# A fused attention and gated-MLP layer: the V weights on a second load queue, and the order of TensorE's first twelve microseconds

## Chip, cores and metric

The kernel runs on one core of one Trainium2 chip. The metric is the device time of one execution in microseconds (us), taken as the median of several runs. A profiled execution adds a trace, in which times are counted from the start of the span.

The engines are named as in the profile: PE is TensorE (matrix multiply; PEld is its weight load), DVE is VectorE, ACT is ScalarE, POOL is GpSimd, SP is SyncE. SPq and ACTq are the DMA issues made by SP and by ACT.

## What is computed

One input block `x` of 2048 rows by 512 columns (bf16) is layer-normalized. Two branches start from the normalized rows `xn`, and their results are added to `x`:

```python
def _A_ref(x, wqkv, wo):
    B, S, D = x.shape
    H = 32; Dh = D // H; W = 256
    qkv = (x @ wqkv).reshape(B, S, 3, H, Dh).transpose(2, 0, 3, 1, 4)
    q, k, v = qkv[0], qkv[1], qkv[2]
    scores = einsum("bhqd,bhkd->bhqk", q, k) * (Dh ** -0.5)
    idx = jnp.arange(S)
    mask = (idx[:, None] - idx[None, :] >= 0) & (idx[:, None] - idx[None, :] < W)
    p = softmax(where(mask, scores, -1e9))
    o = einsum("bhqk,bhkd->bhqd", p, v)
    return o.transpose(0, 2, 1, 3).reshape(B, S, D) @ wo

def _B_ref(x, w_gate, w_up, w_down):
    return ((x @ w_gate) * (x @ w_up)) @ w_down      # 1792 hidden columns

xn = layernorm(x)
out = x + _A_ref(xn, A_wqkv, A_wo) + _B_ref(xn, B_w_gate, B_w_up, B_w_down)
```

(The einsum and transpose wrappers of the reference are written out here.) The attention has 32 heads of 16 columns and a sliding window of 256 rows.

## The kernel before

**Tiling.** The 2048 rows are 16 blocks of 128, grouped in four chunks `T` of 512. Every product over the 512 input columns is a sum of four matmuls over 128 columns each (`k` = 0 to 3). For that the normalized block must stand with its columns in the partitions: `xnT`. In chunk 0 the four blocks are transposed by PE (four transposes of 128 by 128 a block into a PSUM tile `xTp`, which ACT copies to `xnT`, `norm_transpose`, L219 to L234); later chunks use DMA transposes.

**Order.** The program is written out in a fixed order, and each engine executes its own instructions in that order. `setup` (L82) issues all loads on SP's queue, in this order: x block 0, x block 1, x blocks 2 and 3 in one DMA, then the V, K and Q thirds of `Wqkv` (512 KB each), then halves of the gate and up weights, and so on. PE runs 40 matmuls on a zeroed tile `idle` meanwhile (`keep_busy`, L147); nothing reads their result.

`first_chunk` (L292) is the head of the kernel. For each block DVE computes the mean and variance (`norm_stats`, L193 and L194), POOL the reciprocal root (`norm_scale`, L206; DVE adds the epsilon for block 0, POOL for the others), and DVE the normalized block `xn` (`norm_apply`, L214). DVE's order is: statistics of blocks 0 and 1, normalization of 0, statistics of 2, normalization of 1, statistics of 3, normalization of 2. Then PE transposes block 0 and runs eight idle matmuls, and a loop over `b` transposes block `b + 1` and computes the V product of block `b` (`proj_v`, L258: four matmuls into one PSUM tile `vp`, then a copy to `V` by DVE, or by ACT for block 2). The normalization of block 3 is written after the V product of block 0, so that on DVE it comes behind that block's copy. After the loop come the first K and Q products (`proj_qk`, L275).

**The rest.** A loop over 64-row score pieces follows: scores on PE (L350), exponentials on ACT (L353), masks on POOL and DVE, sums over the values on PE (L473). Between these, gate and up products (L502, L513) and the projections of the next chunk are put as filler (`fill`); `PADS` adds no-ops to PE's stream after two of the steps, at most three to a piece of filler. Chunks 1 to 3 each begin with three gate and up pairs, then `down_phase`, which computes the down and output products of the chunk before (`psd`, L535 and L541) between wide score pieces (`B`).

**PSUM banks.** Eight banks hold matmul results. Banks 4 to 7 hold a score tile. The first four are handed out in rotation by `m_tile` (L77): `at_bank` is the next one. `down_phase` closes all and opens one bank for `psd` and three for `B`: `psd` gets bank 0 for the first block if `at_bank` is 0, else bank 3, and changes sides with each block:

```python
        late, high = None, 0 if self.at_bank == 0 else 1
        self.close_banks(5)
        for b in range(4):
            for name in ("ps_b", "ps_d") if b % 2 != high else ("ps_d", "ps_b"):
```

Of the kernel before, what the change touches and what calls it, by code (L numbers as in the profile page):

```python
# [7 lines left out]
BF16 = mybir.dt.bfloat16  # L8
# [28 lines left out]
class Kernel:  # L37
# [44 lines left out]
    def setup(self):  # L82
        nc, const, NT, NF = self.nc, self.const, self.NT, self.NF
        self.x = const.tile([128, NT, 512], BF16, name="x")
        self.Wqkv = const.tile([128, 4, 1536], BF16, name="Wqkv")
        self.Wo = const.tile([128, 4, 512], BF16, name="Wo")
        self.Wg = const.tile([128, 4, self.F], BF16, name="Wg")
        self.Wu = const.tile([128, 4, self.F], BF16, name="Wu")
        self.Wd = const.tile([128, NF, 512], BF16, name="Wd")
        xv = self.x_d.rearrange("(t p) d -> p t d", p=128)  # L90
        wq = self.w_d["qkv"].rearrange("(k p) n -> p k n", p=128)
        wg = self.w_d["g"].rearrange("(k p) n -> p k n", p=128)
        wu = self.w_d["u"].rearrange("(k p) n -> p k n", p=128)
        for lo, hi in ((0, 1), (1, 2), (2, 4)):
            nc.sync.dma_start(out=self.x[:, lo:hi, :], in_=xv[:, lo:hi, :])
        for lo in (1024, 512, 0):
            nc.sync.dma_start(out=self.Wqkv[:, :, lo:lo + 512], in_=wq[:, :, lo:lo + 512])
        h = self.F // 2
        for lo in (0, h):
            nc.sync.dma_start(out=self.Wg[:, :, lo:lo + h], in_=wg[:, :, lo:lo + h])  # L100
            nc.sync.dma_start(out=self.Wu[:, :, lo:lo + h], in_=wu[:, :, lo:lo + h])
            if lo == 0:
                nc.sync.dma_start(out=self.x[:, 4:8, :], in_=xv[:, 4:8, :])
        nc.sync.dma_start(out=self.Wd[:], in_=self.w_d["d"].rearrange("(f p) n -> p f n", p=128))
        wo = self.w_d["o"].rearrange("(c p) n -> p c n", p=128)
        for c in range(4):
            nc.sync.dma_start(out=self.Wo[:, c, :], in_=wo[:, c, :])
        for lo, hi in ((8, 10), (10, 12), (12, NT)):
            nc.sync.dma_start(out=self.x[:, lo:hi, :], in_=xv[:, lo:hi, :])

        self.idle = const.tile([128, 128], BF16, name="idle")
        nc.vector.memset(self.idle[:], 0.0)
        self.keep_busy(40)
        warm = const.tile([128, 1], F32, name="warm")
        nc.vector.memset(warm[:], 0.0)
        nc.scalar.activation(out=warm[:], in_=warm[:], func=ACT.Exp)
        ident = const.tile([128, 128], BF16, name="ident")
        nc.gpsimd.memset(ident[:], 0.0)
        nc.gpsimd.affine_select(out=ident[:], in_=ident[:], compare_op=ALU.not_equal, fill=1.0,
                                base=0, pattern=[[-1, 128]], channel_multiplier=1)  # L120
        self.ident = ident
        pi = const.tile([128, 1], I32, name="pi")
        nc.gpsimd.iota(pi[:], pattern=[[0, 1]], base=0, channel_multiplier=1)
        podd = const.tile([128, 1], I32, name="podd")
        nc.vector.tensor_scalar(out=podd[:], in0=pi[:], scalar1=4, scalar2=1,
                                op0=ALU.arith_shift_right, op1=ALU.bitwise_and)
        self.odd = const.tile([128, 1], F32, name="odd")
        nc.vector.tensor_copy(out=self.odd[:], in_=podd[:])
        self.even = const.tile([128, 1], F32, name="even")
        nc.vector.tensor_scalar(out=self.even[:], in0=self.odd[:], scalar1=-1.0, scalar2=1.0,  # L130
                                op0=ALU.mult, op1=ALU.add)
        self.mhalf = const.tile([128, 4], F32, name="mhalf")
        nc.gpsimd.memset(self.mhalf[:], -0.5)
        self.diag = const.tile([128, 64], BF16, name="diag")
        self.far = const.tile([128, 64], BF16, name="far")
        nc.gpsimd.memset(self.diag[:], BIG)
        nc.gpsimd.memset(self.far[:], BIG)
        for half in (slice(0, 64), slice(64, 128)):
            self.triangle(self.diag[half], True)
            self.triangle(self.far[half], False)  # L140
        self.xnT, self.Q, self.hT, self.OT = {}, {}, {}, {}
        self.K, self.V, self.VS = {}, {}, {}
        self.strips, self.parts, self.at = {}, {}, {}
        self.stock = []
        self.new_values()
# [73 lines left out]
    def norm_transpose(self, t, by_dma):  # L219

        nc = self.nc
        xn = self.xns.pop(t)
        T, b = divmod(t, 4)
        if b == 0:
            self.xnT[T] = self.chunk2.tile([128, 4, 4, 128], BF16, tag="xnT", name=f"xnT{T}")
        if by_dma:
            nc.sync.dma_start_transpose(out=self.xnT[T][:, b, :, :], in_=xn[:])
            return
        n = 2 if b == 0 else 4
        for lo in range(0, 4, n):  # L230
            ps = self.m_tile([128, n, 128], BF16, "xTp")
            for k in range(n):
                nc.tensor.transpose(ps[:, k, :], xn[:, 128 * (lo + k):128 * (lo + k) + 128], self.ident[:])
            nc.scalar.activation(out=self.xnT[T][:, b, lo:lo + n, :], in_=ps[:], func=ACT.Copy)  # L234
# [57 lines left out]
    def first_chunk(self):  # L292

        self.new_chunk(0)
        for b in range(2):
            self.norm_stats(b, 1)
            self.norm_scale(b, 1)
        for b in (0, 1, 2):
            self.norm_apply(b)
            if b < 2:  # L300
                self.norm_stats(b + 2, 1)
                self.norm_scale(b + 2, 1)
        self.norm_transpose(0, False)
        self.keep_busy(8)
        for b in range(4):
            if b < 3:
                self.norm_transpose(b + 1, False)
            self.proj_v(b, engine="act" if b == 2 else "dve")
            if b == 0:
                self.norm_apply(3)  # L310
        self.proj_qk(0, 0, 1, engine="dve")
        self.proj_qk(0, 0, 0, engine="act")
        self.swap_halves(0, self.nc.scalar)
        self.proj_qk(0, 1, 1, engine="dve")
# [491 lines left out]
```

## Time and profile before

| | us |
|---|---|
| Median of 3 runs | 262.15 (262.0 to 262.67) |
| The profiled execution, its own time | 262.46 |
| Its span | 260.6 |
| First x block: issued / statistics start | 0.79 / 3.03 |
| First transposes on PE (block 0) | 5.30 |
| First K product on PE, recorded start | 11.08 |

The span is the time from the first to the last recorded instruction; the execution's own time is 1.86 us longer. A PE record starts before its turn in the array, because matmuls are pipelined; in the chain of waits each piece begins where the one before it ends, so the same work stands there some 0.15 us later (the first K product at 11.24). Busy shares are averages over the whole span. What the change touches lies in the first twelve microseconds, so the timeline and the chain of that stretch are the views to read, together with each load's time from issue to landing.

### The profile page before, as it was taken

What the parts mean: (1) busy time and instruction counts of PE and PEld (TensorE: products, weight loads), DVE (VectorE), ACT (ScalarE), POOL (GpSimd) and SP (SyncE); (2) the same over time, 40 slices, a digit from 0 to 9 for tenths busy, and PEclk for the clock granted to TensorE, in tenths of its full rate; (3) what the DMA queues carried; (4) which work ended last, traced back from release to release, by engine and by line L of the source; (5) the groups of instructions that cost most, each with busy time, mean ns of one, the idle gap of its engine ahead of it and who ended that gap; (6) DMA issues with size and microseconds to landing.
All of it is one profiled execution on the core that took longest, in us unless ns stands there. A gap on an engine that the chain in (4) does not pass through costs nothing.

```text
span 260.6 us, 7774 instructions
## 1 busy us (share of the span) xinstructions
PE 256.4 (98%) x3170; PEld 120.1 (46%) x3170; DVE 169.0 (65%) x342; ACT 183.4 (70%) x167; POOL 114.7 (44%) x278
## 2 busy tenths in 40 slices
PE   8999999999999999999999999999999999999995
PEld 8444444444444544444544454444544445444453
DVE  6687898888836487347976468642895235948144
ACT  3377788888586788787756768879874877877500
POOL 6216242425356745343445764334242565543500
DMA  6999910120013220002001301000200100000002
GB/s 207 377 353 336 283 27 20 24 48 1 3 40 43 60 25 1 3 0 48 3 3 41 82 24 23 0 4 1 48 5 4 36 23 24 3 0 3 3 0 83
DMA packets 19426, 15.04 MB, mean 58 GB/s; under 512 B 7360, under 2 KB 19392, under 8 KB 19392
## 3 DMA queue, kind: packets, MB, share of 16 engines
q1 hardware_dynamic: 18848, 14.26, 19.7%
q8 instruction: 26, 0.43, 0.7%
q10 hardware_dynamic: 544, 0.30, 0.4%
q14 instruction: 8, 0.07, 0.1%
HBM read 9.70 MB, written 2.10 MB: 45 GB/s over the span
## 4 chain that ended last, share of the span: by engine, by line
PE 91%; DVE 7%; issue 1%
PE up L513 17%; PE gp L502 17%; PE psd L535 16%; PE qkp L275 10%; PE S L350 8%; PE acc L473 6%; PE vp L263 6%; PE psd L541 5%; PE L L535 2%; PE wps L151 2%; DVE at L479 2%; DVE hT L518 1%; DVE on L492 1%; PE B L350 1%; PE L L541 1%
## 5 line engine op out<-in xcount | busy, mean ns | idle before, releaser
L182 POOL TENSOR_SCALAR_AFFINE_SELECT P<-P 64x256 bf16<-64x256 bf16 x224 | 98.7, 441 | 122.4 <-ACT P L353 110.7
L353 ACT ACTIVATE P<-S 128x2048 bf16<-128x2048 f32 x66 | 123.8, 1876 | 23.3 <-PE S L350 22.4
L502 PE MATMUL gp<-xnT,Wg 128*128 128x512 bf16 x224 | 59.1, 380 | 0.0
L513 PE MATMUL up<-xnT,Wu 128*128 128x512 bf16 x224 | 59.0, 380 | 0.0
L518 DVE TENSOR_TENSOR hT<-up,gsb 128x512 bf16<-128x512 f32 x56 | 38.0, 683 | 24.7 <-ACT gsb L254 12.7
L535 PE MATMUL psd<-Wd,hT 128*128 128x512 bf16 (+1 forms) x210 | 47.8, 369 | 0.0
L448 DVE TENSOR_TENSOR P<-P,diag 128x512 bf16<-128x512 bf16 (+1 forms) x75 | 30.1, 401 | 16.0 <-ACT P L353 15.9
L254 ACT ACTIVATE gsb<-gp 128x512 bf16<-128x512 f32 x49 | 28.5, 596 | 9.5 <-PE gp L502 9.4
L535 PEld LDWEIGHTS <-hT 128*128 128x128 bf16 x238 | 21.6, 98 | 25.5 <-issue 3.1
L513 PEld LDWEIGHTS <-Wu 128*128 128x128 bf16 x224 | 20.6, 98 | 25.6 <-issue 2.7
L502 PEld LDWEIGHTS <-Wg 128*128 128x128 bf16 x224 | 20.5, 98 | 25.5 <-issue 2.9
L353 ACT ACTIVATE P<-B 128x1536 bf16<-128x1536 f32 (+2 forms) x18 | 17.8, 1022 | 17.7 <-PE B L350 10.8
L275 PE MATMUL qkp<-xnT,Wqkv 128*128 128x512 bf16 x128 | 29.8, 380 | 0.0
L350 PE MATMUL S<-Q,K 32*128 32x320 bf16 (+4 forms) x624 | 28.7, 255 | 0.0
L350 PEld LDWEIGHTS <-K 32*128 32x128 bf16 x720 | 11.4, 92 | 27.4 <-issue 26.5
L551 DVE TENSOR_TENSOR x<-psd,x 128x512 bf16<-128x512 f32 (+1 forms) x15 | 9.9, 665 | 20.8 <-PE psd L541 20.8
L479 DVE STREAM_TRANSPOSE at<-acc 128x512 f32<-128x512 f32 x30 | 19.1, 688 | 4.6 <-PE acc L473 4.6
L275 PEld LDWEIGHTS <-Wqkv 128*128 128x128 bf16 x128 | 11.8, 98 | 14.7 <-issue 1.6
L473 PE MATMUL acc<-P,VS 64*32 64x320 bf16 (+4 forms) x672 | 17.6, 253 | 0.0
L473 PE MATMUL acc<-P,V 64*32 64x320 bf16 (+4 forms) x672 | 17.2, 253 | 0.0
L473 PEld LDWEIGHTS <-VS 64*32 64x32 bf16 x720 | 15.4, 91 | 2.2 <-issue 1.5
L263 PE MATMUL vp<-Wqkv,xnT 128*128 128x512 bf16 x64 | 15.3, 380 | 0.0
(56 smaller groups left out, 191.3 us busy)
## 6 DMA issues: line engine op xcount, KB each, us to landing
out_dram<-x SPq DMA_DIRECT2D x15, 128.0 KB, 1.7
Wg<-in_B_w_gate_dram SPq DMA_DIRECT2D x2, 896.0 KB, 11.3
Wu<-in_B_w_up_dram SPq DMA_DIRECT2D x2, 896.0 KB, 12.4
Wd<-in_B_w_down_dram SPq DMA_DIRECT2D x1, 1792.0 KB, 16.7
Wqkv<-in_A_wqkv_dram SPq DMA_DIRECT2D x3, 512.0 KB, 6.3
x<-in_A_x_dram SPq DMA_DIRECT2D x2, 512.0 KB, 8.8
VS<-V SPq DMA_DIRECT2D x6, 144.0 KB, 2.6
x<-in_A_x_dram SPq DMA_DIRECT2D x3, 256.0 KB, 6.7
```

The costliest lines, as they stand in the source:

```text
L182: nc.gpsimd.affine_select(out=v, in_=v, pattern=pattern + [[1 if diag else -1, 64]], compare_op=ALU.is_ge if diag else ALU.is_gt, fill=0.0 ...
L254: nc.scalar.activation(out=out, in_=in_, func=ACT.Copy)
L263: nc.tensor.matmul(ps[:], lhsT=self.xnT[T][:, b, k, :], rhs=self.Wqkv[:, k, 1024:1536], start=(k == 0), stop=(k == 3))
L275: nc.tensor.matmul(ps[:], lhsT=self.Wqkv[:, k, lo:lo + 128], rhs=self.xnT[T][:, :, k, :], start=(k == 0), stop=(k == 3))
L350: self.nc.tensor.matmul(kw.pop("out"), start=True, stop=True, skip_group_check=True, **kw)
L353: self.nc.scalar.activation(out=out, in_=in_, func=ACT.Exp, scale=0.25)
L448: self.nc.vector.tensor_tensor(out=v, in0=v, op=ALU.min, in1=self.diag.unsqueeze(1).unsqueeze(1).to_broadcast([128, 4, n, 64]))
L473: nc.tensor.matmul(accs[par][32 * e:32 * e + 32, q:q + n], lhsT=v, rhs=P[rows, e, col:col + n], start=(i == 0), stop=(i == len(todo) - 1), ...
L502: nc.tensor.matmul(ps[:], lhsT=self.Wg[:, k, 128 * f:128 * f + 128], rhs=self.xnT[T][:, :, k, :], start=(k == 0), stop=(k == 3))
L513: nc.tensor.matmul(ps[:], lhsT=self.Wu[:, k, 128 * f:128 * f + 128], rhs=self.xnT[T][:, :, k, :], start=(k == 0), stop=(k == 3))
L518: nc.vector.tensor_tensor(out=self.hT[T, f][:], in0=ps[:], in1=self.gsb[:], op=ALU.mult)
L535: nc.tensor.matmul(ps, lhsT=self.hT[T, f][:, 128 * b:128 * b + 128], rhs=self.Wd[:, f, c0:c1], start=(f == 0), stop=False)
```

## The change

The V third of `Wqkv` (512 KB, one DMA) is issued by ACT instead of SP. A one-column memset by DVE into that third stands ahead of it, which the DMA has to wait for. The tile `idle` and its memset move to the start of `setup`, so that the order of DVE's memsets is `idle`, then the column, then `warm`.

In the head, eight idle matmuls after block 0's transposes become four. The V product of block 0 is split: its matmuls for `k` = 0 and 1 come ahead of block 1's transposes, those for 2 and 3 behind. Of block 2's V product, the matmul for `k` = 0 comes ahead of block 3's transposes. Block 3's transposes go to two tiles of two instead of one of four, so that ACT copies them in two instructions. After the V products of blocks 1 and 2, four no-ops each are put into PE's stream.

```diff
@@ setup @@
+        self.idle = const.tile([128, 128], BF16, name="idle")
+        nc.vector.memset(self.idle[:], 0.0)
         xv = self.x_d.rearrange("(t p) d -> p t d", p=128)
...
         for lo, hi in ((0, 1), (1, 2), (2, 4)):
             nc.sync.dma_start(out=self.x[:, lo:hi, :], in_=xv[:, lo:hi, :])
-        for lo in (1024, 512, 0):
+        nc.vector.memset(self.Wqkv[:, 0, 1024:1025], 0.0)
+        nc.scalar.dma_start(out=self.Wqkv[:, :, 1024:1536], in_=wq[:, :, 1024:1536])
+        for lo in (512, 0):
             nc.sync.dma_start(out=self.Wqkv[:, :, lo:lo + 512], in_=wq[:, :, lo:lo + 512])
...
-        self.idle = const.tile([128, 128], BF16, name="idle")
-        nc.vector.memset(self.idle[:], 0.0)
         self.keep_busy(40)
@@ norm_transpose @@
-        n = 2 if b == 0 else 4
+        n = 2 if b in (0, 3) else 4
@@ first_chunk @@
         self.norm_transpose(0, False)
-        self.keep_busy(8)
+        self.keep_busy(4)
         for b in range(4):
+            first = {0: (0, 1), 2: (0,)}.get(b, ())
+            if first:
+                self.proj_v(b, first)
             if b < 3:
                 self.norm_transpose(b + 1, False)
-            self.proj_v(b, engine="act" if b == 2 else "dve")
+            self.proj_v(b, range(len(first), 4), engine="act" if b == 2 else "dve")
             if b == 0:
                 self.norm_apply(3)
+            for _ in range(4 if b in (1, 2) else 0):
+                self.nc.tensor.nop("pad", nofuse=True)
         self.proj_qk(0, 0, 1, engine="dve")
```

## The prediction

> **What bounds the kernel now.** I read the busy shares first, then the chain that ended last, then its first 12 us.
>
> ```profile
> PE 256.4 (98%) x3170; PEld 120.1 (46%) x3170; DVE 169.0 (65%) x342; ACT 183.4 (70%) x167; POOL 114.7 (44%) x278
> PE 91%; DVE 7%; issue 1%
> ```
>
> TensorE (PE) is both the busiest engine and 91% of the chain. From 9.5 us to 257 us it never stands still except for 0.1 us twice, near 134 and 197 us, where it waits for VectorE (DVE). So PE time saved at the head arrives at the end almost whole, and nothing but the head can be shortened. The chain there, in order of time (start, us, what):
>
> ```profile
> 5.49 0.43 PE xTp L233 x4
> 5.91 0.85 PE wps L151 x8
> 6.77 0.38 PE xTp L233 x4
> 7.15 0.86 PE vp L263 x4
> 8.01 0.22 PE xTp L233 x4
> 8.23 0.88 PE vp L263 x4
> 9.11 0.01 issue
> 9.12 0.40 PE xTp L233 x4
> 9.52 1.73 PE vp L263 x8
> 11.24 2.59 PE qkp L275 x12
> ```
>
> I call the transposes of block b Tb and its value sum Vb. Idle matmuls stand between T0 and T1; T3 at 9.12 costs 0.40 where T2 cost 0.22, because it waited for its block from DVE. The head ends at 11.24. The idle matmuls are filler, but DVE is hardly less busy (timeline: start, length, operation):
>
> ```profile
> 5.16 0.68 DVE L193 BATCH_NORM_STATS2 st<-x 128x6 f32<-128x512 bf16 x1
> 6.01 0.41 DVE L214 TENSOR_SCALAR xn<-x,mv,rs 128x512 bf16<-128x512 bf16 x1
> 7.19 0.41 DVE L214 TENSOR_SCALAR xn<-x,mv,rs 128x512 bf16<-128x512 bf16 x1
> 8.05 0.69 DVE L256 CAST V<-vp 128x512 bf16<-128x512 f32 x1 [0.45 <-PE vp L263]
> 8.65 0.41 DVE L214 TENSOR_SCALAR xn<-x,mv,rs 128x512 bf16<-128x512 bf16 x1
> ```
>
> Block 2's statistics start at 5.16, block 1 is normalized at 6.42, block 2 at 7.60; block 3 stands in line behind V0's copy and is done at 9.06, which is what T3 waited for. Third view, the loads (size, us from issue to landing):
>
> ```profile
> x<-in_A_x_dram SPq DMA_DIRECT2D x1, 256.0 KB, 2.9
> Wqkv<-in_A_wqkv_dram SPq DMA_DIRECT2D x1, 512.0 KB, 4.1
> ```
>
> The first is blocks 2 and 3 of x, issued at about 1.66: landed at 4.56, 0.60 before their use. The second is the V weights, issued at 2.18: landed at 6.28.
>
> **Four idle matmuls out.** Eight take 0.85, so four give 0.43 at that place.
>
> **Half of V0 ahead of T1.** T1 cannot start before 6.47 anyway (block 1 at 6.42 plus 0.05, as from 5.24 to 5.29 at T0), so the order is now T0 to 5.91, idle to 6.34, half of V0, T1, the rest of V0. V0's first half needs xnT's first half: ScalarE (ACT) starts at 5.74, 0.38 each, so 6.12: in time. It runs slowly, though. The idle matmuls come 0.106 apart and T2's transposes 0.055 apart, both of 128 columns; the last transpose of T1 took 268 ns between 314 before and 219 after. So TensorE ran at half speed until about 7.05. The full-speed 0.43 of V0's half therefore lasts from 6.34 to 7.12, T1 to 7.34, V0 to 7.77, against 8.01 before. The Trainium skill (TensorE: Matmul & The Clock Gate, Part 1 on the HAM clock gate) says that the array runs at half clock until it has been busy for a window of about 3.4 us, and that the window runs free of the kernel; this trace agrees with the factor and shows one opening, 6.0 us after the first matmul. By that page the opening could come up to about 7.9 in another execution and V0's end with it some 0.4 later, and in the kernel before it would delay V0 as well; the sum does not use it.
>
> **After V0.** V0's copy moves from 8.05 to 7.81 (DVE is free at 7.60), block 3 is normalized by 8.82, and T3 no longer waits. T2 follows at 7.77 to 7.99. V1 needs xnT of block 1: T1's end 7.34, ACT 0.60 and handovers, 8.02. So V1 8.02 to 8.89, V2's first quarter to 9.11, T3 to 9.33, the rest of V2 to 9.98, V3 to 10.85. **At best the head is 0.39 shorter.** T3's copy in two halves takes 0.66 on ACT as block 0's did (one piece: 0.60), over at about 10.0; its first half is there at 9.7, before V3. If that cover went, V3 would wait 0.06 or so.
>
> **V's load on ACT's queue.** One DMA leaves SyncE's (SP's) queue, so the K and Q weights and all behind them are issued 0.5 earlier; they landed at about 9.0 and 10.4 against uses at 11.1 and 12.1, and Wg at 12.9 against 18.9. All have more than a microsecond of cover. ACT now issues one DMA ahead of its table load: 0.47 to 0.67 (the issues on SP and ACT), which ends table load (1.28) and warm-up (0.20) near 3.2 instead of 2.28; the next ACT work is at 5.74. What is behind that wait is thus covered by 2.5 us. The added DVE memset (0.06, like the other small one) lies in DVE's idle time before 1.49 and lets V's issue start at about 1.0, against 2.18. V then lands before 6.28, and is needed at 6.34.
>
> The price is what V's bytes do to x's. The x blocks' 524 KB were over by about 4.1 in the rates per half microsecond (2.0 to 4.5: 203, 293, 141, 340, 240 GB/s; then 350 and 393). The landing came 0.46 after the last byte. If V takes an equal share from 2.0 on at those rates, x's last byte comes at 5.55 and the blocks land at 6.0 instead of 4.56: 0.85 later than DVE starts on them now (block 0 itself would land 0.36 late, which this swallows). Lower end: two queues together reach the later 375 GB/s, the blocks land by 5.1 and nothing is late. Between: the engines' busy share was 0.58, 1.05, 0.82, 1.00, 0.91 in those half microseconds, so some 0.35 us of engine time was free, which V could use; that leaves 0.56. I take **0.3**, midway between on time and this, because the rate rose to 393 GB/s with rows of the same 1 KB once more was queued. Call the lateness d: block 2 is ready at 7.60 + d, T2 starts at 7.65 + d and takes 0.40 as T3 did when it waited, and the head ends at 10.88 + d. Queued behind the waiting statistics on DVE is block 1's normalization too, but T1 now starts at 7.12 instead of 6.56 and bears a d of 0.6. **Gain 0.36 - d, here 0.06.** The Trainium skill (DMA: Bandwidth & Descriptors, Rules for kernel authors) says that spreading loads over issuing engines brings no bandwidth, since all run on the same 16 DMA engines and interleave, and only issue time is saved. It speaks against this edit; no row before shows two load queues at once. By the rule d is near 0.85 and the kernel is 0.5 slower, by the later rate of the rows it is 0.36 to 0.39 faster.
>
> **Eight no-ops.** Upper bound, if the array waits for each: an idle pair is two instructions in 0.106, so 0.42 for eight. Lower bound: 120 and 178 such no-ops already go three to a piece of filler after 97 and 160 us, and the chain there still has 0.86 for every four matmuls. I take zero; they follow four matmuls of 0.216, and the queue is ahead. They replace eight instructions taken out, so the stream keeps its length.
>
> **Banks.** T3's second tile shifts the rotation of four PSUM banks by one. The next bank is 0 at each down phase now (73 tiles from bank 3, then 48 each); it will be 1, `high` becomes 1, and block 0's `psd` goes to bank 3, last used by the last gate tile, instead of to the oldest.
>
> ```profile
> 68.81 0.60 ACT L254 ACTIVATE gsb<-gp 128x512 bf16<-128x512 f32 x1
> 69.39 1.89 PE L535 MATMUL psd<-Wd,hT 128*128 128x512 bf16 x8
> ```
>
> That bank is free at 69.41, psd starts at 69.39: cost 0 to 0.1. In the second phase the copy ends at 132.20 before a start at 132.27, and B's wait at 134.28 for DVE hides the rest. I take 0.05, so the total is a gain of about 0.0.
>
> **The sum.** The profiled execution took 262.46 (span 260.6, 1.86 around it), 0.3 above the median 262.15, and within the runs shown (262.0 to 262.67). Sum: -0.36 + 0.3 + 0.05 = 0.0. I set **262.1**.
>
> **The rivals.** (1) *Blocks on time*: two queues fill the slow start, d = 0. For it: 141 to 293 GB/s early against 375 later. Against: busy shares near 1 most of that time. Change -0.39 + 0.05: 261.8; with T3's 0.18 and all of 0.43 it could not pass 0.61, 261.5. (2) *The slower side*: V's bytes go ahead of blocks 2 and 3, which land when V did, 6.28 or later. DVE waits at the statistics of block 2, T2 behind it. d = 1.12 gives +0.76 and with the banks 262.95; another 0.2 from a slow half microsecond like that of 141 GB/s, 263.15. It decides from d = 0.36, a landing after 5.52, and passes 0.3% from a landing at about 6.3. (3) *V's load does not start early*, the table load holding ACT to 2.07: V then shares with K from 3.0, lands near 6.7, V0 ends at 7.98 and only T3's wait is saved: -0.2, 261.95.
>
> **Chances.** 0.3% is 0.79 us, about what a measurement of this kernel can tell from no change. Forecast (landing 5.3 to 6.0, 261.9 to 262.6) 0.42; blocks on time 0.23; slower side 0.27; V late 0.08. Faster by over 0.3% lies past rival 1's own bound and needs the spread of the runs (0.67) or something unseen: 0.17. Slower by over 0.3% is most of rival 2: 0.24. Same: 0.59. The range takes in both bounds and part of the spread: 261.1 to 263.2.
>
> **What would show it.** T0 starting where it did; block 2's statistics between 5.2 and 5.8 with a DMA wait before them (right) or at 5.16 (rival 1) or after 6.2 (rival 2); no wait before T3; qkp starting at about 11.2; psd's first start in the down phases within 0.1 of gsb's end. The prediction is wrong if qkp starts outside 10.7 to 12.1, or if the time moves while qkp's start does not.

## The result, and the profile after

The changed kernel takes 264.68 us (median of four runs, 264.44 to 264.90) against 262.08 before: the ratio is 1.0091, 95% interval 1.0079 to 1.0104. That is 2.6 us slower than before, 2.6 above the forecast (262.1) and 1.5 above the upper end of its range (263.2). The profiled execution took 264.44 with a span of 262.6, so the two profiled executions differ by 2.0; what follows explains these 2.0.

The page of the changed kernel, busy shares and chain, first. "DMA" is new in the chain, with 2%:

```profile
PE 255.5 (97%) x3150; PEld 120.0 (46%) x3166; DVE 169.3 (64%) x343; ACT 183.7 (70%) x168; POOL 114.5 (44%) x278
PE 88%; DVE 7%; DMA 2%; issue 2%; SPq 0%
```

The head's chain of the changed kernel (start, us, what):

```profile
1.24 4.34 DMA x<-in_A_x_dram
5.60 0.71 DVE st L195
6.33 0.18 DVE mv L196
6.51 0.31 DVE xn L216
6.87 0.61 PE xTp L235 x4
7.48 0.43 PE wps L153 x4
7.90 0.45 PE vp L265
8.35 0.22 issue
8.57 0.63 PE xTp L235 x4
9.20 0.85 PE vp L265 x2
10.05 0.22 PE xTp L235 x4
10.27 1.08 PE vp L265 x5
11.35 0.22 PE xTp L235 x4
11.57 1.51 PE vp L265 x7
13.09 2.64 PE qkp L277 x12
```

It begins with a load, and that load is **block 1 of x**: issued at 1.24, landed at 5.58, 4.34 later. Its statistics start at 5.60 instead of 4.04, and on DVE the normalization of block 0 stands behind them, so PE stands still from 5.49 to 6.87 and its first transposes start at 6.87 instead of 5.30. Block 1's statistics before and after, and PE's first transposes after (in brackets the idle time ahead, and what ended it):

```profile
4.04 0.68 DVE L193 BATCH_NORM_STATS2 st<-x 128x6 f32<-128x512 bf16 x1
5.60 0.69 DVE L195 BATCH_NORM_STATS2 st<-x 128x6 f32<-128x512 bf16 x1 [1.64 <-DMA x<-in_A_x_dram]
6.87 0.61 PE L235 MATMUL xTp<-ident,xn 128*128 128x128 bf16 x4 [1.38 <-DVE xn L216]
```

Then a second thing shows: two of V's matmuls take 0.85 at 9.20, though four took 0.86 before. The array is at half speed until about 9.9; before, by the matmuls' spacing, it left that state at about 7.05. The trace also records the clock that the array is granted, from the first change on: in the changed kernel that record begins at 9.91, with full speed. (Ahead of the first entry the views show 1.00, whatever the speed.) The first K product comes at 13.09 instead of 11.24.

Where the bytes went, by load queue, between 2.5 and 3.5 us: packets, MB, busy share of 16 engines. q1 is SP's queue and q10 is ACT's. Before:

```profile
DMA packets 235, 0.22 MB, mean 217 GB/s; under 512 B 23, under 2 KB 235, under 8 KB 235
q1 hardware_dynamic: 235, 0.22, 93.5%
```

And in the changed kernel:

```profile
DMA packets 77, 0.08 MB, mean 79 GB/s; under 512 B 0, under 2 KB 77, under 8 KB 77
q10 hardware_dynamic: 74, 0.08, 53.1%
q1 hardware_dynamic: 3, 0.00, 1.1%
```

SP's queue, on which blocks 1 to 3 of x wait, moved three packets in that microsecond. V's queue was not fast either: both together moved a third of what one queue moved before. The loads' times from issue to landing say the same (block 1 before; then, in the changed kernel, blocks 2 and 3; block 1, as the later of the 128 KB loads; V):

```profile
x<-in_A_x_dram SPq DMA_DIRECT2D x1, 128.0 KB, 2.2
x<-in_A_x_dram SPq DMA_DIRECT2D x1, 256.0 KB, 5.0
x<-in_A_x_dram SPq DMA_DIRECT2D x1, 128.0 KB, 4.3
Wqkv<-in_A_wqkv_dram ACTq DMA_DIRECT2D x1, 512.0 KB, 4.9
```

V, issued at 1.04, landed at 5.9, 0.3 earlier than before. Block 1 landed 2.2 us later than before and blocks 2 and 3 2.1 us later.

After the head little changes. The score pieces of both kernels, set side by side, stand 1.89 apart from the first to the end of chunk 0, 1.98 apart from the first down phase on, and 1.98 to 2.01 to the end.

### The profile page after: what moved, and what is told of

Same layout as the page of the kernel before. It is cut to its first block, busy times and chain, and to the rows that moved or that the text cites. A ratio compares the mean times of both kernels' runs of the same rounds, so it can differ in the third digit from the quotient of the medians.

```text
span 262.6 us, 7760 instructions
## 1 busy us (share of the span) xinstructions
PE 255.5 (97%) x3150; PEld 120.0 (46%) x3166; DVE 169.3 (64%) x343; ACT 183.7 (70%) x168; POOL 114.5 (44%) x278
## 4 chain that ended last, share of the span: by engine, by line
PE 88%; DVE 7%; DMA 2%; issue 2%; SPq 0%
PE up L520 17%; PE gp L509 17%; PE psd L542 15%; PE qkp L277 10%; PE S L357 8%; PE acc L480 6%; PE vp L265 6%; PE psd L548 5%; PE L L542 2%; DVE at L486 2%; DMA x<-in_A_x_dram 2%; DVE hT L525 1%; DVE on L499 1%; PE B L357 1%; PE xTp L235 1%
## 5 line engine op out<-in xcount | busy, mean ns | idle before, releaser
L542 PE MATMUL psd<-Wd,hT 128*128 128x512 bf16 (+1 forms) x200 | 46.8, 368 | 0.9 <-issue 0.5
## 6 DMA issues: line engine op xcount, KB each, us to landing
Wg<-in_B_w_gate_dram SPq DMA_DIRECT2D x2, 896.0 KB, 10.7
```

The source lines that it names most:

```text
L542: nc.tensor.matmul(ps, lhsT=self.hT[T, f][:, 128 * b:128 * b + 128], rhs=self.Wd[:, f, c0:c1], start=(f == 0), stop=False)
```

## The experiments

Each is an edit of the changed kernel ("after") or of the kernel before; times are medians, ratios are to the kernel before on the same chip.

**V back on SP.**

```diff
-        nc.vector.memset(self.Wqkv[:, 0, 1024:1025], 0.0)
-        nc.scalar.dma_start(out=self.Wqkv[:, :, 1024:1536], in_=wq[:, :, 1024:1536])
-        for lo in (512, 0):
+        for lo in (1024, 512, 0):
```

> The changed kernel with V's load back on SP behind the x blocks (no column memset); the new order on PE, the four idle matmuls, the two tiles of block 3 and the no-ops stay. Theory 'V's load delays block 1 of x, and all else follows from it': block 1's statistics start near 4.0 again, the first K product near 10.9 in the chain, and the time is 261.6 to 262.1. Rival 'the new order itself costs, because V's first half now runs at half speed': block 1 is on time and the time still stays 1 us or more above before, 263 to 264.5.

Measured 262.60, ratio 1.0011 (1.0001 to 1.0021). Block 1 is on time (statistics at 3.87), and the loss is gone but for 0.1%. The first K product is at 10.94 in the chain, 0.30 earlier than before, as expected; but in this execution the array was at full speed from 3.97 on, against about 7.05 in the profile before, so the new order need not be all of it. The time is not lower, though. The score pieces show why: 0.25 ahead after the head, 0.17 ahead after the first down phase, 0.14 behind from 94 us on. At that place the chain of this run has

```profile
93.26 0.65 PE up L518 x3
93.91 0.13 issue
94.04 0.39 PE up L518
```

where four such matmuls take 0.86 elsewhere: a pause in the middle of one product that waits for no engine. Later runs look at it. The large loss belongs to V's load.

**The queue alone.** The kernel before with only these lines of the change:

```diff
-        for lo in (1024, 512, 0):
+        nc.vector.memset(self.Wqkv[:, 0, 1024:1025], 0.0)
+        nc.scalar.dma_start(out=self.Wqkv[:, :, 1024:1536], in_=wq[:, :, 1024:1536])
+        for lo in (512, 0):
```

> The kernel before with V's load on ACT's queue (and the column memset), nothing else changed. Theory: block 1 of x lands about 2 us late, block 0's transposes start near 6.9 instead of 5.3, PE goes back to half speed, and the time is 264 to 265: the whole loss of the change or a little more, since V's sum is not cut in two. Rival 'the new order itself costs': 262 to 263.

Measured 264.13, ratio 1.0076 (1.0048 to 1.0104), with single runs from 263.35 to 265.98. Block 1's statistics start at 5.23. In the profiled run (263.58) the array was at full speed from 3.87 on and stayed there, though PE then stood still for 1.70 us; the first K product is only 0.94 late. So the queue alone brings most of the loss, and the size varies from run to run. Between 2.5 and 3.5 us SP's queue was again left out, while V's moved almost as much as the one queue did before:

```profile
DMA packets 192, 0.20 MB, mean 196 GB/s; under 512 B 1, under 2 KB 192, under 8 KB 192
q10 hardware_dynamic: 191, 0.20, 81.4%
q1 hardware_dynamic: 1, 0.00, 0.1%
```

So it is the order in which the queues are served that makes block 1 late here, and not a low rate.

**V later on ACT, first try.** The DMA is written behind ACT's warm-up instead of behind a memset.

```diff
         nc.scalar.activation(out=warm[:], in_=warm[:], func=ACT.Exp)
+        nc.scalar.dma_start(out=self.Wqkv[:, :, 1024:1536], in_=wq[:, :, 1024:1536])
```

> The changed kernel with V's load still on ACT's queue, but written behind ACT's warm-up, so that it is issued near 2.3 instead of 1.04, after all three x loads; no column memset. Theory 'the load that is issued ahead is served ahead': x lands as before (block 1 by 3.5, blocks 2 and 3 by 4.7), V lands at 6.5 to 7.2 and may hold V's first half a little; the time is 261.7 to 262.4. Rival 'two load queues share the engines, whatever the order': blocks 2 and 3 land at 5.5 or later and the time is 262.6 to 263.5.

Measured 264.33, ratio 1.0073 (1.0056 to 1.0089). It told nothing apart, because V was issued no later. ACT's timeline of this run:

```profile
0.79 1.28 ACT L116 ACT_TABLE_LOAD   x1 [0.79 <-PEq L796]
1.05 0.48 ACTq L117 DMA_DIRECT2D Wqkv<-in_A_wqkv_dram  x1
```

The engine was loading its table until 2.07, yet the issue, which stands behind it in the program, went out at 1.05. It also ends my third rival: the table load does not hold the issue.

**Banks.** After, with block 3's transposes in one tile again:

```diff
-        n = 2 if b in (0, 3) else 4
+        n = 2 if b == 0 else 4
```

> The changed kernel with block 3's transposes in one tile of four again, so that the rotation of banks is that of before; V's load stays on ACT's queue. Theory: only the small loss in the first down phase (0.05 to 0.15) goes away, the time is 264.4 to 264.7. Rival 'the shifted banks are a good part of the loss': 262.5 to 264.0.

Measured 264.75, ratio 1.0083 (1.0059 to 1.0107), single runs from 263.38 to 265.69: too spread for 0.1 us. The score pieces show the size. Set against the changed kernel this run is 0.52 behind ahead of the first down phase and 0.44 behind after it, so the shifted banks cost 0.08 there and nothing later. The 0.5 of the head is the array again. It had reached full speed at 4.20, PE stood still for 1.78 us, and the array fell back to half speed from 7.61 to 11.02. In the view by stretches the granted clock is the third number from the end:

```profile
7.00:7.50 0.50, 0.36 (x7) 0.19 (x5) 0.47 (x3) 0.47 (x2) 0.39 (x1) 1.00 1.11 348
7.50:8.00 0.50, 0.48 (x1) 0.18 (x3) 0.50 (x2) 0.19 (x1) 0.36 (x1) 0.61 1.09 346
10.50:11.00 0.50, 0.50 (x3) 0.15 (x1) 0.24 (x1) 0.25 (x1) 0.00 (x0) 0.50 1.04 373
11.00:11.50 0.50, 0.50 (x3) 0.20 (x2) 0.00 (x0) 0.00 (x0) 0.00 (x0) 0.98 1.06 384
```

**V later on ACT, second try.** The two lines of V's load moved behind DVE's last small setup operation (`even`):

```diff
             nc.sync.dma_start(out=self.x[:, lo:hi, :], in_=xv[:, lo:hi, :])
-        nc.vector.memset(self.Wqkv[:, 0, 1024:1025], 0.0)
-        nc.scalar.dma_start(out=self.Wqkv[:, :, 1024:1536], in_=wq[:, :, 1024:1536])
...
                                 op0=ALU.mult, op1=ALU.add)
+        nc.vector.memset(self.Wqkv[:, 0, 1024:1025], 0.0)
+        nc.scalar.dma_start(out=self.Wqkv[:, :, 1024:1536], in_=wq[:, :, 1024:1536])
```

> The changed kernel with V's load still on ACT's queue, but made to wait (the column memset stands behind DVE's last small setup operation, which ended at 2.01), so that it is issued near 2.1, when SP has issued all three x loads. The run before this one that meant to do it still issued V at 1.05, since ACT's queue does not wait for the work ahead of it on the engine. Theory 'what is issued ahead is served ahead': block 1 of x lands by 3.5, blocks 2 and 3 by 4.8, V between 6.2 and 7.0; head as with V on SP or up to 0.5 longer, time 262.3 to 263.0. Rival 'two load queues share the engines, whatever the order': blocks 2 and 3 land after 5.3, first K product after 11.5 in the chain, time 263.0 or more.

Measured 264.05, ratio 1.0057 (1.0036 to 1.0078). V was issued at 2.06. The x loads were served as before (block 1's statistics at 3.99, blocks 2 and 3 landed 2.8 after issue), so an issue ahead of theirs, not the second queue itself, made x late. But V then shared the engines with the K and Q weights on SP, and landed 6.0 after its issue. PE's timeline:

```profile
5.48 0.39 PE L153 MATMUL wps<-idle 128*128 128x128 bf16 x4
8.24 0.59 PE L265 MATMUL vp<-Wqkv,xnT 128*128 128x512 bf16 x1 [2.37 <-DMA Wqkv<-in_A_wqkv_dram]
```

PE waited 2.37 us for V. That case was in neither expectation. In this profiled execution (266.83, the slowest of its runs) the array had been at full speed from 3.97, fell back to half speed from 7.38 to 14.21, and PE's fourth set of transposes at 12.88 still took 0.63.

**Half of V ahead.**

```diff
-        nc.scalar.dma_start(out=self.Wqkv[:, :, 1024:1536], in_=wq[:, :, 1024:1536])
+        nc.scalar.dma_start(out=self.Wqkv[:, 0:2, 1024:1536], in_=wq[:, 0:2, 1024:1536])
+        nc.sync.dma_start(out=self.Wqkv[:, 2:4, 1024:1536], in_=wq[:, 2:4, 1024:1536])
```

> The changed kernel with only half of V's load (k = 0 and 1, 256 KB) on ACT's queue at 1.04, and the other half on SP behind the x loads. Theory 'V's bytes go ahead of block 1': half the bytes ahead make block 1 land about 0.7 us earlier than with all of V ahead, at 4.5 to 5.0 instead of 5.1 to 5.6, and the time is 263.0 to 263.9. Rival 'a second queue in use costs a fixed delay, whatever it carries': block 1 lands at 5.1 or later, time 264 or more.

Measured 263.08, ratio 1.0030 (1.0016 to 1.0044). Block 1's statistics start at 4.54. With no V ahead of it they start near 4.0 and wait for nothing; with 512 KB ahead they start at 5.23 to 5.62 in six profiles. The lateness grows with the bytes ahead; a fixed delay for using a second queue is ruled out.

**PE kept busy, two ways.** First, after with 13 more idle matmuls ahead of block 0's transposes:

```diff
-        self.keep_busy(40)
+        self.keep_busy(53)
```

> The changed kernel with 53 idle matmuls instead of 40 ahead of block 0's transposes, so that PE stays busy while it waits for block 1 of x. Theory 'a second part of the loss is that the array stays at half speed after 1.6 us of standing still': x lands as late as in the changed kernel, but the array is at full speed by about 7.1, V's matmuls are 0.22 apart, the first K product comes 0.7 to 1.2 us earlier than 13.09, and the time is 263.2 to 263.9. Rival 'the lateness of block 1 is all': no change, 264.3 to 264.9.

Measured 265.70, ratio 1.0119 (1.0102 to 1.0136): slower than the change. Yet the first K product came at 12.47, as expected. In this execution the array was at full speed from 4.45 on, so the 53 idle matmuls were over early and PE still stood still for 1.11 us. The time was lost elsewhere, near 94 us on PE:

```profile
93.58 0.26 PE L357 MATMUL S<-Q,K 32*128 32x192 bf16 x2
95.11 0.39 PE L357 MATMUL S<-Q,K 32*128 32x192 bf16 x6 [1.28 <-issue]
```

So the test was repeated with 40 idle matmuls, the last 14 of which have 256 columns: meant to fill the wait at half speed, with not one instruction more (`keep_busy` takes a width, `idle` is 256 wide, and the last argument keeps the same PSUM tile).

```diff
-        self.keep_busy(40)
+        self.keep_busy(26)
+        self.keep_busy(14, 256, False)
```

> The changed kernel with the last 14 of its 40 idle matmuls 256 columns wide, so that PE is busy until about 6.9 with no instruction more than before. The run with 13 idle matmuls more brought the first K product from 13.09 to 12.47, but its stream was 26 instructions longer and PE then stood still for 1.28 us near 94 us. Theory 'half speed after standing still is a part of the loss by itself': the first K product again comes 0.5 to 0.9 earlier than 13.09, nothing like 1.28 us near 94 us, time 263.6 to 264.2. Rival 'keeping PE busy does not pay': 264.4 or more.

Measured 263.81, ratio 1.0065 (1.0049 to 1.0080), against 1.0091 for the change. Block 1 is as late as in the changed kernel (statistics at 5.62), but the chain is

```profile
9.24 0.40 PE xTp L238 x4
9.64 1.08 PE vp L268 x5
10.72 0.22 PE xTp L238 x4
10.95 1.51 PE vp L268 x7
12.46 2.64 PE qkp L280 x12
```

at full speed, and the first K product is 0.63 earlier than in the changed kernel. No pause stands near 94 us. But PE was not kept busy in this execution (the first line gives the size of the first of the 40):

```profile
1.10 4.44 PE L155 MATMUL wps<-idle 128*128 128x128 bf16 x40 [1.10 <-DVE warm L118]
6.88 0.40 PE L238 MATMUL xTp<-ident,xn 128*128 128x128 bf16 x4 [1.34 <-DVE xn L219]
```

The array was at full speed from 3.84 on, the idle matmuls ran through faster, and PE stood still for 1.34 us, as long as in the changed kernel (1.38), without falling back. So this profile shows what half speed costs when block 1 is equally late, 0.63. It does not show that filling the wait wins it back. The times (263.68 to 264.10, against 264.44 to 264.90 for the change, on another chip) fit that but do not settle it: the first try at a later V, with the same head as the change, has single runs from 263.50 to 264.89.

**One tile, V on SP.** As the first experiment, with block 3 in one tile:

```diff
-        nc.vector.memset(self.Wqkv[:, 0, 1024:1025], 0.0)
-        nc.scalar.dma_start(out=self.Wqkv[:, :, 1024:1536], in_=wq[:, :, 1024:1536])
-        for lo in (512, 0):
+        for lo in (1024, 512, 0):
...
-        n = 2 if b in (0, 3) else 4
+        n = 2 if b == 0 else 4
```

> V's load on SP, the new order on PE, block 3's transposes in one tile of four, so that the rotation of banks is that of before. Theory 'the head gains 0.25 us, the shifted banks cost 0.08, the rest of what V on SP lost is a pause of 0.3 in PE's stream near 94 us that isn't the same in every build': the head is 0.15 to 0.3 shorter than before, nothing is lost at the first down phase, the time is 262.0 to 262.4. Rival 'the new order costs further down': 262.5 or more.

Measured 262.79, ratio 1.0011 (0.9999 to 1.0024). The head was not shorter: the first K product is at 11.27. V landed at 6.4 and its first half waited for it, and V's last sum waited at 10.24 for the copy of block 3, which comes in one piece here. Nothing was lost at the first down phase, and there was no pause near 94 us.

**The pause by itself.** The kernel before, with 26 no-ops behind the head's V sums and 26 fewer behind step 27.

```diff
-PADS = {27: 120, 47: 178}
+PADS = {27: 94, 47: 178}
...
+        for _ in range(26):
+            self.nc.tensor.nop("pad", nofuse=True)
         self.proj_qk(0, 0, 1, engine="dve")
```

> The kernel before with 26 no-ops behind the head's V sums and 26 fewer behind step 27: same loads, same order, same number of instructions in all. Theory 'a block of PE's instructions arrives about 2.4 us after it is asked for, and where 26 instructions more stand ahead, PE reaches that place 1.3 us too early': the head as before within 0.1, one pause of 0.9 to 1.4 near 92 to 94 us, time 263.2 to 263.9. Rival 'the pause came with the late loads': as before, 262.1 to 262.6. Rival 'no-ops cost by themselves': the head 0.5 us or more longer.

Measured 265.24, ratio 1.0130 (1.0099 to 1.0161). The pause came, with every load on SP as before:

```profile
92.95 0.26 PE L352 MATMUL S<-Q,K 32*128 32x192 bf16 x2
94.71 0.39 PE L352 MATMUL S<-Q,K 32*128 32x192 bf16 x6 [1.50 <-issue]
```

The last rival holds too: the score pieces after the head are 0.89 late, so 26 no-ops in a row cost some 0.03 each here. (The profile puts this wait down to DVE's copy of V, but in the kernel before the same K product starts ahead of the end of that copy.)

**V on SP, stream and banks as before.** The first experiment without the eight no-ops (eight more behind step 27), and with the rotation of banks begun one earlier:

```diff
-PADS = {27: 120, 47: 178}
+PADS = {27: 128, 47: 178}
...
-        self.usual_banks(3)
+        self.usual_banks(2)
...
-            for _ in range(4 if b in (1, 2) else 0):
-                self.nc.tensor.nop("pad", nofuse=True)
```

> V's load on SP, the new order on PE with two tiles for block 3, the rotation of banks started one bank earlier so that it ends up as before, and the eight no-ops left out of the head (eight more are put behind step 27, so that the stream further down is aligned as before). Theory: head 0.25 shorter, nothing lost at the first down phase, and no pause near 94 us, because the instruction that waits for the next block of the stream comes four matmuls later: 261.8 to 262.2 where before has 262.1 to 262.5, 0.2 to 0.3 faster in the profile. Rival 'the pause near 94 us has nothing to do with the place in the stream': a pause of up to 0.3 stays, no gain over before.

Measured 262.60, ratio 1.0019 (1.0001 to 1.0037). No pause near 94 us and no loss at the down phase, as expected; but the head is 0.12 late at the first score piece, because V landed at 6.69 (4.52 after 2.17) and its first half, due at 6.34, waited:

```profile
2.17 4.52 DMA Wqkv<-in_A_wqkv_dram
6.69 0.14 issue
6.82 0.38 PE vp L263
```

**V in halves on SP.** The same with V's load cut in two DMAs, k = 0 and 1 first:

```diff
-        nc.vector.memset(self.Wqkv[:, 0, 1024:1025], 0.0)
-        nc.scalar.dma_start(out=self.Wqkv[:, :, 1024:1536], in_=wq[:, :, 1024:1536])
+        for k in (0, 2):
+            nc.sync.dma_start(out=self.Wqkv[:, k:k + 2, 1024:1536], in_=wq[:, k:k + 2, 1024:1536])
```

> As the run with fewer instructions (V on SP, new order on PE, banks and stream aligned as before), but V's load cut in two DMAs on SP, k = 0 and 1 ahead of k = 2 and 3. In that run V landed at 6.69, and V's first half, moved up to 6.34, waited for it; in the two runs with V whole on SP it landed at 6.3 and 6.6. Theory 'with V behind x, the half of V moved up comes too close to V's landing': the first half lands before 6.0, the head is 0.2 to 0.35 shorter than before, and the time is 261.8 to 262.1 where before has 262.2. Rival 'more DMAs delay the K and Q weights or the rest': the gain of the head is lost by the first score piece, 262.3 or more.

Measured 262.36, ratio 1.0005 (0.9995 to 1.0015). The first half landed in time, 3.6 after 2.18, but the second only at 7.48, 4.79 after its issue, and V's second half waited for that. The score pieces are 0.04 ahead. The expected 0.2 to 0.35 did not come, and no version tried beats the kernel before.

## Why the prediction was wrong

**What bounds the kernel** held: what the head loses arrives at the end, 1.85 of 2.0.

**V's load on ACT's queue is the step that failed.** The term is the lateness d. I took 0.3 and allowed 0.85 at most; block 2's statistics started at 6.73 instead of 5.16, so d was 1.57. The prediction's own 10.88 + d then gives 12.45 for the end of the head, and the other 0.64 up to 13.09 is the array's half speed, for which the sum had no term. The sign of being wrong (a first K product outside 10.7 to 12.1) came true.

The step had the right danger, and the Trainium skill's rule (DMA: Bandwidth & Descriptors, Rules for kernel authors), that a second issuing engine brings no bandwidth, is borne out: from 2.0 to 4.5 us the five half-microsecond rates average 243 GB/s before and 236 in the changed kernel. Three things were wrong in what I made of it.

- *The wrong block.* I priced the lateness d at the statistics of blocks 2 and 3, took a late block 0 as swallowed by it, and gave a late block 1 no price. The load that V passes first is block 1: SP issues it at 1.24, V was issued at 1.04. Its statistics stand on DVE ahead of the normalization of block 0, so the very first transposes wait, with PE idle for 1.38.
- *The wrong bounds.* The upper end assumed an equal share at the rates of before. In fact the queue that issued first was served almost alone between 2.5 and 3.5 us, in the changed kernel at a third of the former rate, with the queue alone at nine tenths of it. My slower rival had V's bytes go ahead, but of blocks 2 and 3 only; it was the right mechanism at the wrong place, and its 262.95 fell short by 1.7.
- *A cover taken as fixed.* I took the opening of the array's clock at 7.05 from one trace and left it there. By the records of the granted clock it opened between 3.8 and 4.5 in seven of the experiments' profiles, ahead of PE's long wait, and between 5.7 and 6.6 in four that have V on SP and no long wait ahead of the opening. In the two where PE stood still while the array was at half speed (the changed kernel, 1.38 us, and the first try at a later V, 1.21) it opened only at 9.91 and 9.70. So the opening differs from execution to execution, and came late where the wait came first. Where the opening came first, it outlived waits of up to 1.70 us and was lost in the two profiles with the longest, 1.78 (banks) and 2.37 (V later, second try). Half speed cost 0.63. The Trainium skill (TensorE: Matmul & The Clock Gate, Part 1) asks for some 3.4 us of sustained work in a window that runs free of the kernel. From 6.87 to 9.91 are 3.0 us, with 0.22 of standing still in them, which is somewhat less; the two stretches of half speed that the granted clock shows whole last 3.41 and 6.83 us, which agrees. I had cited that rule for the work put into the slow stretch, and not for the case that PE stops.

The parts add up to the difference of the spans, 2.0: block 1 late with the array at full speed 1.22 (12.46 against 11.24, net of what the new order saves), half speed 0.63, banks 0.08, the rest below 0.1.

**The other steps.** The new order with x on time was worth 0.30 at the first K product (forecast 0.36 to 0.39) in the one profile where V landed at 6.3 and the array was at full speed early; how much of it is the order is not shown. V's landing on SP varied between 6.3 and 6.7 in the runs with V whole on SP, and the half of V that moved up to 6.34 has no slack left. Block 3's two tiles were needed: without them V3 waited. The banks cost 0.08 (forecast 0.05). The eight no-ops cost nothing visible: the five V matmuls around four of them take 1.08, which is 0.216 each. The table load was covered, as said. The third rival (V's issue held by the table load) was wrong.

**What stays open.** The medians differ by 2.6, the profiled executions by 2.0; the profiled one was the slowest but one of the kernel before (0.4 above its median) and the fastest of the changed one (0.2 below). In the two slower runs of the changed kernel, 264.79 and 264.90, the mean granted clock is 0.994, the same as in the profile of the test of the banks, where the array fell back for 3.41 us. That they fell back too is likely, and not shown; the 0.4 on the other side is not explained. Why the queue that issued 0.2 us earlier left the other almost nothing, and why both together moved so little between 2.5 and 3.5 us in the changed kernel, was not found.

## What to carry to other kernels

A load moved to another queue is not free of those it leaves behind: compare its issue time with each load on the other queues, and for every one that it passes, look up what stands behind its first use on the consuming engine. Time that PE saves at the start is worth nothing if it then has to stand still there, and the array can stay at half speed, or fall back to it: 3.0 us in the changed kernel, 3.4 and 6.8 in two others. Before judging a small edit, check that the instruction stream further down still stands where it stood.

## What was unexpected

PE's stream pauses at one place whatever the program has there. In four profiles the pause comes behind the same number of PE instructions in the trace, 2236: V on SP (0.13), the queue alone (0.04), 13 idle matmuls more (1.28) and 26 no-ops (1.50). Each time the load of a 16 KB piece of instructions starts 2.4 to 2.6 us before PE goes on, and ends 1.4 us before: with V on SP it runs from 91.64 to 92.60 and PE goes on at 94.03, with 26 no-ops from 92.07 to 93.28 and PE goes on at 94.70. In the kernel before the same load starts at 91.3, and PE passes the place at 93.7 to 94.1 without a visible pause; 26 instructions more ahead of it make that a pause of 1.3 to 1.5 us. The run without the eight no-ops in the head had none. That PE waits for this piece is what fits all of these, and is inferred. The no-ops of the change keep the stream's length, so its own profile shows only 0.03 there.

ACT's queue issues a DMA while the engine is still executing what stands ahead of it in the program (1.05 against a table load that ended at 2.07). To hold a DMA back, it needs something to wait for.
